# Tails of three weight matrices and of their gradients handled in pairs of slices, in an attention and gated-unit backward kernel

## The chip, the cores and the metric

The kernel runs on one core of one Trainium2 chip. A core has a matrix engine (PE, whose weight loads the profile calls PEld), a vector engine (DVE), a scalar engine (ACT), GpSimd (POOL), and SyncE (SP), which here only issues transfers. 16 DMA engines move data between the chip's memory (HBM) and the core's on-chip buffers. A tile in SBUF has 128 partitions; matrix products land in PSUM and have to be copied out of it by ACT or DVE. The metric is the time in device microseconds of one execution; the median of three runs is compared.

## The reference

One decode step (one token, two sequences) of an attention block and a bilinear gated unit that run side by side on the same normalised input, and the gradients of all of it. `D` is 576, there are 32 query heads and 16 key/value heads of 128, 4096 cached positions, and 4608 hidden columns in the gated unit.

```python
def _A_ref(x, k_cache, v_cache, wq, wo):
    q = (x @ wq).reshape(B, Sq, Hq, Dh).transpose(0, 2, 1, 3)
    k = jnp.repeat(k_cache, rep, axis=1)
    v = jnp.repeat(v_cache, rep, axis=1)
    scores = jnp.einsum("bhqd,bhkd->bhqk", q, k) * (Dh ** -0.5)
    p = _softmax(scores, axis=-1)
    o = jnp.einsum("bhqk,bhkd->bhqd", p, v)
    return o.transpose(0, 2, 1, 3).reshape(B, Sq, Hq * Dh) @ wo
def _B_ref(x, w_gate, w_up, w_down):
    g = jnp.einsum("bsd,df->bsf", x, w_gate)
    u = jnp.einsum("bsd,df->bsf", x, w_up)
    return jnp.einsum("bsf,fd->bsd", g * u, w_down)
...
xn = _layernorm(A_x)
out = A_x + _A_ref(xn, A_k_cache, A_v_cache, A_wq, A_wo) + _B_ref(xn, B_w_gate, B_w_up, B_w_down)
```

The kernel returns `out` and the gradients, for a given `grad_out`, of `x`, both caches, `wq`, `wo`, `w_gate`, `w_up` and `w_down`. The caches and their gradients are by far the largest: 33.6 MB each, in bf16. In all 92.5 MB are read and as much is written.

## The kernel before

**Attention.** The 16 key/value heads are taken in 8 groups of two heads; a group with its two sequences makes two steps, 16 in all. A step loads two K tiles and two V tiles of 1 MB (`load_kv`, L997), transposes them in 32x32 blocks on DVE into tiles called X (`turn`, L421), takes scores and the softmax (`softmax`, `dscore`), contracts with the untransposed tiles (`contract`), and makes the gradients of K and V as outer products, which are cast out of PSUM into 1 MB tiles and stored (`head_outer`; the casts are `cp`, L425 on ACT and L427 on DVE; the store is `put`, L652, issued by SP). K and V tiles, X tiles and store tiles all come out of one ring of 16 tiles, `big`, with a cap for each use: 8 for K and V, 13 for X, 5 for stores.

**Weights of a group.** `load_w` loads four heads' columns of `wq` (512 columns) and rows of `wo` into tiles `ww`. `wq` has 576 rows, that is four blocks of 128 and a tail of 64. The blocks are one transfer of 512 KB (L1015). The tail's 64 rows by 512 columns are split into two halves of 256 columns, one on partitions 0 to 63 and one on 64 to 127 of the same `ww` tile (L1011, 64 KB; for group 0 on SP's queue, else on POOL's). `group_front` multiplies them with the normalised input, `xs`. `xs` holds the input's tail twice, with zeros in the other half (blocks 4 and 5), so that a tile with something else on its other half can be multiplied with it. `group_back`, after both steps of the group, makes the gradients of `wo` (`rows_outer`) and of `wq` (`cols_outer` for the 512 rows, `tail_outer` for the 64 of the tail) and transposes `wq` (L955, one instruction over 2304 columns taken as 1152 32-bit ones) to find what flows back to the input (`dxn`, L630 and L635; added into `accx`, L964).

**Gated unit.** `mlp` runs over nine slices of 512 columns, 0 to 8. A slice's `gu` tile holds four blocks of gate, four of up, and one block in which partitions 0 to 63 hold gate's tail and 64 to 127 up's (L1033, two transfers of 64 KB, besides two of 512 KB at L1030; all on POOL's queue). There is one `gu` buffer; it is released (L824) when the slice's columns have been transposed for the flow back to the input, the tail among them into `Xt`. `w_down` goes to a `ww` tile on SP's queue (L1037).

**Gradients of the tails.** `tail_outer` has one or two right-hand sides. For gate and up it puts gate on partitions 0 to 63 and up on 64 to 127 of a `tl` tile (two buffers) and stores each with 64 KB (L652); for `wq` only partitions 0 to 63 are used:

```python
def ev(e, o):
    cp(e, st[0:64 * nw, 256 * A:256 * A + 256].rearrange("p (a f) -> p a f", a=2), o[0:64 * nw, :, 0:P])
return mms, (0.053, 0.104), 256, ev
```

Each tail is evicted in two pieces of 256 columns.

**Order.** Nothing is scheduled at run time. While the program is built, `Order` runs every part of the work as a stream that asks for engine time, buffers and transfers, with a modelled duration for each; among streams that could start on an engine within `SLACK` of the first, the one with the lowest priority number goes first. That fixes the order of instructions on each engine, and of the transfers on SP's and POOL's queues. The priority of a stream is `STEP * s + PR[name]`, with additions for the first two steps (`HEAD`) and the last two (`TAIL`); `DMA` models a transfer's time, `CAP` the shares of the ring, `MLP0` and `MLPD` when the slices' weights are loaded, counted in K and V loads, `BIAS` the choice between ACT and DVE for a cast. An instruction that comes up before its data are there waits, and so does all behind it on its engine or queue.

**Start and end.** `front` loads `x` and `grad_out` (2.2 KB each, ACT's queue) into `xy`, a tile of its own that is kept to the end; there `rows_add` and `rows_put` add them to the results of `final_out` and `final_dx` and store these through it (L1327 to L1329).

## Time and profile before

| | before |
|---|---|
| median of 3 runs | 482.37 us (481.89 to 482.74) |
| span of the profiled execution | 482.5 us |
| PE, PEld busy | 377.9 us (78%), 212.1 us (44%) |
| DVE busy | 349.8 us (73%), 658 instructions |
| ACT busy | 345.6 us (72%), 529 instructions |
| POOL busy | 248.5 us (51%), 356 instructions |
| moved by DMA | 185.93 MB in 33,444 packets, 385 GB/s over the span |
| PE clock granted, mean | 0.654 |

The profiled execution is a run of its own; its span differs from the median by 0.1 us, so what is read from it can be set against the runs directly. The page cuts the span into 40 slices of 12 us. The DMA engines' busy tenths in them show at a glance where transfers run (9 is 90% or more), and the line under it how much they moved:

```profile
DMA  8998999999999989999999999999999999999894
GB/s 298 385 404 326 415 392 422 386 384 397 422 412 378 370 332 328 394 417 402 416 403 409 367 401 420 398 412 422 407 396 421 421 413 394 401 399 376 300 410 164
```

A transfer is cut into packets that its 16 engines work through; the packet records give start, length and size of each. The page lists what the queues' transfers were; the median from issue to landing is the last number:

```profile
out_dram<-big SPq DMA_DIRECT2D x64, 1024.0 KB, 12.1
out_dram<-big POOLq DMA_DIRECT2D x26, 512.0 KB, 11.1
out_dram<-tl POOLq DMA_DIRECT2D x26, 64.0 KB, 8.4
gu<-in_B_w_gate_dram POOLq DMA_DIRECT2D x9, 64.0 KB, 11.7
ww<-in_A_wq_dram POOLq DMA_DIRECT2D x7, 64.0 KB, 9.4
```

### The profile page before, as it was taken

The page shows a single profiled execution, that of the slowest core. Times are in us where ns is not written, and L with a number is a line of the kernel's source. Part 1 is how long each engine was busy: PE and PEld are TensorE (multiplying, and loading weights), DVE is VectorE, ACT ScalarE, POOL GpSimd, SP SyncE. Part 2 cuts the span into 40 slices and gives each one's busy share as a digit, 9 for nine tenths or more (in the row PEclk, how much of TensorE's full clock was granted, in tenths as well). Part 3 has the DMA queues.
Part 4 walks back from the last instruction along what each step waited for, and adds up shares of the span by engine and source line. Part 5 has one row for each costly group of instructions (what it writes and reads, how often), then busy time and mean ns, then how long its engine had stood idle before and what let it go on. Part 6 is the DMA issues. An engine that isn't in the chain of part 4 may idle for free. (4 is left out here: it accounts for less than half of the span.)

```text
span 482.5 us, 14582 instructions
## 1 busy us (share of the span) xinstructions
PE 377.9 (78%) x6122; PEld 212.1 (44%) x6122; DVE 349.8 (73%) x658; ACT 345.6 (72%) x529; POOL 248.5 (51%) x356
## 2 busy tenths in 40 slices
PE   0577978668962899879989898787896887598996
PEld 0444545433631544535553554444452544334544
DVE  6678857866766868677577888687676788298872
ACT  6059976578871688976658974789786982498992
POOL 6176803874057663551557624865715863265601
PEclk9999585675855656655555755767575765568575
DMA  8998999999999989999999999999999999999894
GB/s 298 385 404 326 415 392 422 386 384 397 422 412 378 370 332 328 394 417 402 416 403 409 367 401 420 398 412 422 407 396 421 421 413 394 401 399 376 300 410 164
DMA packets 33444, 185.93 MB, mean 385 GB/s; under 512 B 5034, under 2 KB 5170, under 8 KB 16994
## 3 DMA queue, kind: packets, MB, share of 16 engines
q1 hardware_dynamic: 18714, 131.22, 67.8%
q0 software_dynamic: 14656, 53.77, 29.5%
q8 instruction: 48, 0.79, 0.6%
q14 instruction: 18, 0.15, 0.1%
q10 hardware_dynamic: 8, 0.00, 0.0%
HBM read 92.48 MB, written 92.48 MB: 383 GB/s over the span
## 5 line engine op out<-in xcount | busy, mean ns | idle before, releaser
L425 ACT CAST big<-ps_o 128x1024 bf16<-128x1024 f32 (+1 forms) x324 | 288.4, 962 | 47.1 <-PE ps_o L1129 33.8
L421 DVE STREAM_TRANSPOSE big<-big 128x1024 f32<-128x1024 f32 x128 | 152.8, 1219 | 15.8 <-DMA out_dram<-big 11.7
L1095 POOL TENSOR_TENSOR BD<-vr,mask 128x2048 bf16<-128x2048 bf16 x32 | 115.3, 3602 | 33.6 <-ACT vr L425 16.6
L1107 PE MATMUL ps_m<-big,W 128*32 128x128 bf16 x2048 | 59.6, 283 | 10.2 <-POOL W L1072 6.1
L427 DVE CAST big<-ps_o 128x1024 bf16<-128x1024 f32 (+1 forms) x52 | 59.5, 1145 | 9.7 <-PE ps_o L1129 3.6
L1129 PE MATMUL ps_o<-BD,pp 32*128 32x512 bf16 x256 | 54.3, 533 | 14.9 <-ACT big L425 6.6
L1107 PEld LDWEIGHTS <-W 128*32 128x32 bf16 x2048 | 47.2, 125 | 28.4 <-issue 19.5
L1129 PE MATMUL ps_o<-BD,dd 32*128 32x512 bf16 x256 | 51.8, 544 | 6.1 <-ACT big L425 5.1
L652 POOL DMA_DIRECT2D out_dram<-big x43 | 33.4, 777 | 39.1 <-ACT big L425 25.3
L1072 POOL COPY W<-rep 32x16 bf16<-32x16 bf16 x128 | 24.5, 192 | 56.1 <-DVE rep L873 51.2
L421 DVE STREAM_TRANSPOSE big<-ww 128x1152 f32<-128x1152 f32 x25 | 34.0, 1358 | 6.2 <-DMA out_dram<-big 5.9
L1284 PE MATMUL ps_m<-big,pp 128*32 128x512 bf16 x256 | 32.2, 607 | 2.2 <-DVE accx L834 1.3
L623 POOL COPY wt<-wm 64x128 bf16<-64x128 bf16 (+1 forms) x34 | 8.9, 261 | 44.6 <-DVE wm L617 43.6
L1129 PEld LDWEIGHTS <-pp 32*128 32x128 bf16 x256 | 12.3, 99 | 39.0 <-issue 34.2
L1284 PE MATMUL ps_m<-big,dd 128*32 128x512 bf16 x256 | 27.1, 512 | 0.8 <-DVE accx L834 0.3
L421 DVE STREAM_TRANSPOSE big<-gu 128x1024 f32<-128x1024 f32 x18 | 21.8, 1224 | 1.6 <-PE ps_m L1107 0.8
L1129 PEld LDWEIGHTS <-dd 32*128 32x128 bf16 x256 | 10.7, 99 | 27.7 <-issue 22.7
L652 POOL DMA_DIRECT2D out_dram<-tl x26 | 14.4, 557 | 15.4 <-ACT tl L425 5.7
L1294 ACT ACTIVATE osb<-ps_m 128x512 bf16<-128x512 f32 x15 | 9.2, 611 | 16.5 <-PE ps_m L1284 16.5
L630 PE MATMUL ps_m<-big,wm 128*32 128x128 bf16 x416 | 14.2, 299 | 5.5 <-DVE big L421 4.4
L672 PEld LDWEIGHTS <-xnr 32*128 32x128 bf16 x416 | 14.4, 111 | 8.0 <-issue 6.4
L672 PE MATMUL ps_o<-hb,xnr 32*128 32x128 bf16 x288 | 15.2, 251 | 2.7 <-ACT big L425 1.4
(210 smaller groups left out, 561.7 us busy)
## 6 DMA issues: line engine op xcount, KB each, us to landing
out_dram<-big SPq DMA_DIRECT2D x64, 1024.0 KB, 12.1
big<-in_A_k_cache_dram SPq DMA_DIRECT2D x28, 1024.0 KB, 13.5
big<-in_A_v_cache_dram SPq DMA_DIRECT2D x28, 1024.0 KB, 18.0
out_dram<-big POOLq DMA_DIRECT2D x26, 512.0 KB, 11.1
out_dram<-big POOLq DMA_DIRECT2D x17, 576.0 KB, 9.4
ww<-in_B_w_down_dram SPq DMA_DIRECT2D x9, 576.0 KB, 15.7
ww<-in_A_wo_dram POOLq DMA_DIRECT2D x8, 576.0 KB, 15.1
gu<-in_B_w_gate_dram POOLq DMA_DIRECT2D x9, 512.0 KB, 12.1
```

The source lines that it names most:

```text
L421: nc.vector.transpose(out, in_)
L425: nc.scalar.copy(out, in_)
L427: nc.vector.tensor_copy(out=out, in_=in_)
L630: nc.tensor.matmul(dp[32 * q:32 * q + 32, 0:P], lhsT=view(Wm[:], 0, P, 8 * pos(q, s), [[1, 32]]), rhs=view(X, 0, P, xoff(q, s), [[xstep, 4 ...
L652: (nc.gpsimd if engine == "POOL" else nc.sync).dma_start(dst, src)
L672: nc.tensor.matmul(o[:, aa, dc * P:(dc + 1) * P], lhsT=xnr[32 * a:32 * a + 32, dc * P:(dc + 1) * P], rhs=rhs(a), start=True, stop=True)
L1072: nc.gpsimd.tensor_copy(view(W_t[t][w][:], 32 * a, 32, 6 + 8 * a, [[G * WW, 4], [WW, G], [1, 2]]), view(rep_t[grp[g]["qs"]][:], 32 * a, 32 ...
L1095: nc.gpsimd.tensor_tensor(BD_t[i][:], view(vr_t[v][:], 0, P, 0, [[0, 16], [1, Dh]]), view(mask16[:], 0, P, 0, [[1, 16], [0, Dh]]), ALU.mult)
L1107: nc.tensor.matmul(sc[32 * cq:32 * cq + 32, :], lhsT=view(W[:], 0, P, (be * G + l) * WW + 6 - 4 * c2 - 2 * l, [[1, 32]]), rhs=view(X[:], 0 ...
L1129: nc.tensor.matmul(o[:, k, :], lhsT=pr2[32 * c4:32 * c4 + 32, :], rhs=BD[32 * c4:32 * c4 + 32, 8 * l + 4 * h2:8 * l + 4 * h2 + 4, :], star ...
L1284: nc.tensor.matmul(ct[32 * j:32 * j + 32, :], lhsT=view(rT, 0, P, 4 * c + 2 * l, [[1, 32]]), rhs=kv_t[kvS[s][t][l]][:, Dh * c:Dh * (c + 4) ...
L1294: nc.scalar.activation(ob, cs, AF.Copy, scale=SCALE)
```

## The change

The tails of `wq`, `w_gate` and `w_up`, and those of their gradients, are no longer handled per slice (or group) but per pair of slices: the even one's 64 rows lie on partitions 0 to 63 and the odd one's on 64 to 127, each with all its 512 columns, in tiles of their own (`gtl` and `wqt` for weights, `tg` and `tq` for gradients). A pair's tails are loaded with the even slice and stored with the odd one, 128 KB a transfer; the ninth slice of the gated unit has no partner and keeps 64 KB. For two right-hand sides `tail_outer` now evicts 64 partitions by 512 columns, not 128 by 256. The transposes of the tails become two instructions each. `Store(9, None, 0)` is a counter that never runs out, since the store is now spawned by `tail_outer` itself. `xy` goes: `x` and `grad_out` are first loaded into a tile of the shared ring, which is released once they have been used, and again near the end (`final_load`), after the last K or V load has been issued, into an X tile. `gs`, `hT` and `gT` have one buffer instead of two. All parameters of the order are others.

```diff
@@ -286,27 +286,26 @@
 def DMA(engine, cost, nbytes, row=8192):
-    packet = 0.0375 * row + 9.0
-    return ("dma", engine, cost, 0.08 + nbytes / 16e3 * packet / row, packet)
+    packet = 0.0364 * row + 8.0
+    return ("dma", engine, cost, 0.02 + nbytes / 16e3 * packet / row, packet)
-CAP = {"kv": 8, "X": 13, "st": 5}
-MLP0, MLPD = 0, 7.51
+CAP = {"kv": 8, "X": 15, "st": 5}
+MLP0, MLPD = 0.53, 7.43
-WQ0, WO0 = 0, 1
+WQ0, WO0 = 0, -2
-BIAS = 0.52
-SLACK = {"PE": 0.07, "ACT": 0.09, "DVE": 0.43, "POOL": 8.93, "SP": 17.19}
+BIAS = 0.572
+SLACK = {"PE": 0.07, "ACT": 0.11, "DVE": 0.33, "POOL": 6.62, "SP": 18.36}
...
@@ -374,16 +373,19 @@
-    gu_t = tiles("gu", NGU, [P, 9 * FS])
+    gu_t = tiles("gu", NGU, [P, 8 * FS])
+    gtl_t = tiles("gtl", 1, [P, 2, FS])
+    wqt_t = tiles("wqt", 2, [P, FS])
     ww_t = tiles("ww", NWW, [P, WB])
-    tl_t = tiles("tl", 2, [P, FS])
+    tg_t = tiles("tg", 1, [P, 2, FS])
+    tq_t = tiles("tq", 1, [P, 1, FS])
-    gs_t = [const.tile([P, 2, P], FP32, name=f"gs{i}") for i in range(2)]
-    hT_t = [const.tile([P, FC, 32], BF16, name=f"hT{i}") for i in range(2)]
-    gT_t = [const.tile([P, 8, 32], BF16, name=f"gT{i}") for i in range(2)]
+    gs = const.tile([P, 2, P], FP32, name="gs")
+    hT = const.tile([P, FC, 32], BF16, name="hT")
+    gT = const.tile([P, 8, 32], BF16, name="gT")
...
@@ -523,10 +525,8 @@
-    xy = const.tile([2, 2 * D], BF16, name="xy")
-
     def front():
-        xb, yb = xy[:, 0:D], xy[:, D:2 * D]
+        xb, yb = st_t[2][0:2, D:2 * D], st_t[2][0:2, 2 * D:3 * D]
...
-        for j in range(1, 4):
+        for j in (1, 3):
             yield REL("st", j)
...
+        yield REL("st", 2)
...
@@ -706,36 +707,49 @@
-    def tail_outer(rhss, dsts, p, events=()):
-        i = yield ACQ("tl")
-        st = tl_t[i]
-        nw = len(rhss)
-        parts = [(d, st[64 * w:64 * w + 64, 0:FS], 64 * FS * 2) for w, d in enumerate(dsts)]
-        store = Store(2, put("POOL", parts, "tl", i, events, 4096), p)
+    def tail_outer(rhss, hh, pair, tag, tl, out, n0, last, p, done):
+        if pair.get(tag) is None:
+            pair[tag] = yield ACQ(tag)
+        i = pair[tag]
+        st, nw = tl[i], len(rhss)
+        if hh:
+            pair[tag] = None
 
         def mk(A):
             def mms(o):
                 for w, rhs in enumerate(rhss):
                     for aa in range(2):
-                        a = 2 * A + aa
-                        nc.tensor.matmul(o[64 * w:64 * w + 64, aa, 0:P], lhsT=xnr[32 * a:32 * a + 32, 512:576],
-                                         rhs=rhs(a), start=True, stop=True)
+                        nc.tensor.matmul(o[64 * hh:64 * hh + 64, aa, P * w:P * (w + 1)],
+                                         lhsT=xnr[32 * (2 * A + aa):32 * (2 * A + aa) + 32, 512:576],
+                                         rhs=rhs(2 * A + aa), start=True, stop=True)
 
             def ev(e, o):
-                cp(e, st[0:64 * nw, 256 * A:256 * A + 256].rearrange("p (a f) -> p a f", a=2), o[0:64 * nw, :, 0:P])
-            return mms, (0.053, 0.104), 256, ev
+                cp(e, view(st[:], 64 * hh, 64, 2 * P * A, [[P, 2], [FS, nw], [1, P]]),
+                   view(o[:], 64 * hh, 64, 0, [[512, 2], [P, nw], [1, P]]))
+            return mms, (0.053 * nw, 0.104), 2 * P * nw, ev
+        if hh:
+            parts = [(d[512:576, n0 - FS:n0 + FS].rearrange("p (h n) -> h p n", h=2), st[:, w, :], P * FS * 2)
+                     for w, d in enumerate(out)]
+        else:
+            parts = [(d[512:576, n0:n0 + FS], st[0:64, w, :], 64 * FS * 2) for w, d in enumerate(out)]
+        ends = [Event(), Event()]
+
+        def one(A):
+            yield from unit(*mk(A), Store(9, None, 0))
+            yield SET(ends[A])
         for A in range(2):
-            yield SPAWN(unit(*mk(A), store), p)
-
-    def mlp(i, Lgu, Ld, gs_slot, wd_slot):
-        gu, wd = gu_t[gs_slot], ww_t[wd_slot]
+            yield SPAWN(one(A), p)
+        yield WAIT(*ends)
+        yield SET(done)
+        if hh or last:
+            yield SPAWN(put("POOL", parts, tag, i, (), 4096)(), p + PR["store"])
+
+    def mlp(i, Lgu, Ld, gs_slot, tl_slot, wd_slot):
+        gu, gtl, wd, hh = gu_t[gs_slot], gtl_t[tl_slot], ww_t[wd_slot], i % 2
         hs = yield ACQ("hb")
-        hb, gs, hT, gT = hb_t[hs], gs_t[hs], hT_t[hs], gT_t[hs]
+        hb = hb_t[hs]
...
@@ -743,10 +757,10 @@
-                k = 4 * w + dc if dc < 4 else 8
+                src = gu[:, FS * (4 * w + dc):FS * (4 * w + dc + 1)] if dc < 4 else gtl[:, w, :]
                 for a in range(4):
-                    nc.tensor.matmul(ug[32 * a:32 * a + 32, 1 - w, :], lhsT=xs[:, dc if dc < 4 else 4 + w, :],
-                                     rhs=gu[:, FS * k + P * a:FS * k + P * (a + 1)], start=(dc == 0), stop=(dc == 4))
+                    nc.tensor.matmul(ug[32 * a:32 * a + 32, 1 - w, :], lhsT=xs[:, dc if dc < 4 else 4 + hh, :],
+                                     rhs=src[:, P * a:P * (a + 1)], start=(dc == 0), stop=(dc == 4))
...
-        yield SPAWN(tail_outer([lambda a, w=w: hb[32 * a:32 * a + 32, 1 + w, :] for w in range(2)],
-                               [out[512:576, f0:f0 + FS] for out in (out_6, out_7)], po, (E[3],)), po)
+        yield SPAWN(tail_outer([lambda a, w=w: hb[32 * a:32 * a + 32, 1 + w, :] for w in range(2)], i % 2, pairs_,
+                               "tg", tg_t, (out_6, out_7), f0, i == NFS - 1, po, E[3]), po)
...
@@ -819,9 +833,12 @@
-        yield DVE(0.4)
-        t32(pairs(Xt[:]), pairs(gu[:, 4096:4608]))
+        for w in range(2):
+            yield DVE(0.37)
+            t32(pairs(Xt[64 * w:64 * w + 64, :]), pairs(gtl[64 * hh:64 * hh + 64, w, :]))
         yield REL("gu", gs_slot)
+        if hh or i == NFS - 1:
+            yield REL("gtl", tl_slot)
...
@@ -846,14 +863,14 @@
-                c0 = dc * FS + h * P if dc < 4 else 4 * FS + (h % 2) * P
-                nc.tensor.matmul(qp[:, h, :], lhsT=wq[:, c0:c0 + P], rhs=xs[:, dc if dc < 4 else 4 + h // 2, 0:2],
+                w = wq[:, dc * FS + h * P:dc * FS + (h + 1) * P] if dc < 4 else wqt[:, h * P:(h + 1) * P]
+                nc.tensor.matmul(qp[:, h, :], lhsT=w, rhs=xs[:, dc if dc < 4 else 4 + g % 2, 0:2],
                                  start=(dc == 0), stop=(dc == 4))
...
@@ -924,7 +941,8 @@
-        yield SPAWN(tail_outer([lambda a: R[32 * a:32 * a + 32, 1, :]], [out_4[512:576, n0:n0 + FS]], po, (E[2],)), po)
+        yield SPAWN(tail_outer([lambda a: R[32 * a:32 * a + 32, 1, :]], g % 2, pairs_, "tq", tq_t, (out_4,), n0, False,
+                               po, E[2]), po)
...
@@ -951,9 +969,15 @@
-        yield DVE(1.37)
-        t32(pairs(X[:, 0:WB]), pairs(wq[:]))
+        yield DVE(1.25)
+        t32(pairs(X[:, 0:4 * FS]), pairs(wq[:, 0:4 * FS]))
         yield REL("ww", st["wq"])
+        hh = 64 * (g % 2)
+        for k in range(2):
+            yield DVE(0.24)
+            t32(pairs(X[64 * k:64 * k + 64, 4 * FS:4 * FS + 256]), pairs(wqt[hh:hh + 64, 256 * k:256 * k + 256]))
+        if hh:
+            yield REL("wqt", st["wqt"])
...
@@ -1007,10 +1033,13 @@
-                yield DMA("POOL" if i else "SP", 0.6, 128 * 256 * 2, 4096 if i else 512)
-                (nc.gpsimd if i else nc.sync).dma_start(ww_t[w][:, 4 * FS:WB],
-                                                        A_wq[512:576, n0:n0 + FS].rearrange("p (h n) -> h p n", h=2))
-                yield ("lset", st["Lq"])
+                if i % 2 == 0:
+                    st["wqt"] = grp[i + 1]["wqt"] = r = yield ACQ("wqt")
+                    yield DMA("POOL" if i else "SP", 0.78 if i else 0.36, 128 * FS * 2, 4096 if i else 1024)
+                    (nc.gpsimd if i else nc.sync).dma_start(
+                        wqt_t[r][:], A_wq[512:576, n0:n0 + 2 * FS].rearrange("p (h n) -> h p n", h=2))
+                    yield ("lset", st["Lq"])
+                    yield ("lset", grp[i + 1]["Lq"])
...
@@ -1024,20 +1053,27 @@
+            if i % 2 == 0:
+                tails["gtl"] = yield ACQ("gtl")
+            gtl = gtl_t[tails["gtl"]]
...
-                yield DMA("POOL", 0.6, 64 * FS * 2, 4096)
-                nc.gpsimd.dma_start(gu[64 * w:64 * w + 64, 8 * FS:9 * FS], Wsrc[512:576, f0:f0 + FS])
+                if i == NFS - 1:
+                    yield DMA("POOL", 0.6, 64 * FS * 2, 4096)
+                    nc.gpsimd.dma_start(gtl[0:64, w, :], Wsrc[512:576, f0:f0 + FS])
+                elif i % 2 == 0:
+                    yield DMA("POOL", 0.78, 128 * FS * 2, 4096)
+                    nc.gpsimd.dma_start(gtl[:, w, :], Wsrc[512:576, f0:f0 + 2 * FS].rearrange("p (h n) -> h p n", h=2))
             yield ("lset", Lgu)
...
-            yield SPAWN(mlp(i, Lgu, Ld, g, d), pr("mlp", (MLP0 + i * MLPD) / 4))
+            yield SPAWN(mlp(i, Lgu, Ld, g, tails["gtl"], d), pr("mlp", (MLP0 + i * MLPD) / 4))
...
+    Exy, xys = Event(), []
+
+    def final_load():
+        yield WAIT(issued[4 * NS - 1])
+        i = yield ACQ("X")
+        xys.append(X_t[i])
+        for n, src in enumerate((A_x, grad_out)):
+            yield DMA("SP", 0.36, 2304, 1152)
+            nc.sync.dma_start(X_t[i][0:2, D * n:D * (n + 1)], src.rearrange("b s d -> (b s) d"))
+        yield ("lset", Exy)
-        yield WAIT(Eprep, *acc_E)
+        yield WAIT(Eprep, Exy, *acc_E)
...
+    od.spawn(final_load(), PR["fin"])
```

Line numbers in the text are those of the kernel before.

## The prediction

> **What bounds the kernel now.** I read the page's queue shares first, then stages of the span, then waits.
>
> ```profile
> q1 hardware_dynamic: 18714, 131.22, 67.8%
> q0 software_dynamic: 14656, 53.77, 29.5%
> q8 instruction: 48, 0.79, 0.6%
> q14 instruction: 18, 0.15, 0.1%
> ```
>
> Columns: packets, MB, share of the 16 DMA engines' span. q1 carries what SP issues, q0 what POOL issues. Together 98.0% of 482.5 us, that is 472.9 us of packet time: the transfers fill the span, while PE, DVE and ACT are busy for 78, 73 and 72%. So the time changes only with packet time or with stretches in which the DMA engines have nothing to do. The stages (busy of PE, PEld, DVE, ACT, POOL, then granted clock, DMA share, GB/s) show where those are:
>
> ```profile
> 0.00:6.00 6.00, 0.00 (x0) 0.00 (x0) 4.86 (x32) 3.80 (x7) 5.38 (x14) 1.00 0.69 215
> 36.00:44.00 8.00, 5.81 (x117) 3.23 (x116) 7.21 (x14) 8.00 (x13) 6.08 (x5) 1.00 0.83 278
> 162.00:180.00 18.00, 16.80 (x264) 9.93 (x264) 13.05 (x26) 11.78 (x22) 10.50 (x9) 0.50 0.89 335
> 440.00:458.00 18.00, 16.12 (x254) 9.38 (x258) 16.59 (x29) 16.42 (x24) 10.94 (x9) 0.65 0.80 310
> 458.00:472.00 14.00, 13.08 (x191) 6.40 (x180) 9.55 (x18) 12.05 (x16) 0.68 (x3) 0.74 1.00 409
> 472.00:482.50 10.50, 6.39 (x69) 4.04 (x68) 2.67 (x12) 3.53 (x6) 2.11 (x3) 0.50 0.36 127
> ```
>
> Length times (1 - DMA share): 1.9, 1.4, 2.0, 3.6, 0 and 6.7 us, in all 15.6 us without transfers. (Elsewhere the share comes to 1.01 or 1.02, since packets of the two queues overlap a little; hence 15.6 rather than 482.5 - 472.9 = 9.6.) The first is the start, the last the closing chain. The three in between, 7.0 us, are what another order can win; the reader should see that ACT and DVE are full in two of them and PE in the third (16.80 of 18 us, at a clock of 0.50).
>
> **1. Packet time.** Tails move in 52 transfers of 64 KB: 26 stores (L652 from tl), 18 loads of gate and up (L1033), 8 of wq (L1011, the first by SP, all others by POOL). The packet records of the trace, taken along each queue in order of issue, give 0.18 us of 16-engine time for a store from tl, 0.20 and 0.18 for the gate and up tails, 0.22 for a wq tail; a 512 KB transfer takes 1.37 to 1.44, an eighth of which is 0.175. The tails take 9.9 us in all; at the wide rate 52 x 0.175 = 9.1. The gain lies between 0 (packets stay at 4 KB) and 0.8; I take 0.4, the middle, as the new shape is in no row. After the change there are 27 such POOL issues (3 + 10 loads, 10 + 4 stores) against 51 before, besides the one by SP. Each POOL issue adds 16 packets of 4 B at 9.4 ns, so 24 x 16 x 9.4 ns / 16 = 0.23 us less. Before each POOL wq tail there are also 112 packets of 32 B at 14.8 ns (0.10 us; 7 times, 0.73 us). If these belong to rows of 512 B, all 0.73 goes; if to the two-half source (h, p, n), which gate and up loads and the pair stores now have too (23 transfers), they become 2.4 us, 1.7 more. I take 0, as L1011 has both traits and cannot tell them apart. Sum -0.6, bounds -1.8 and +1.5.
>
> **2. Fewer POOL issues ahead of the weight loads.**
>
> ```profile
> L652 POOL DMA_DIRECT2D out_dram<-tl x26 | 14.4, 557 | 15.4 <-ACT tl L425 5.7
> L1011 POOL DMA_DIRECT2D ww<-in_A_wq_dram x7: 847/871/887, 36.1 to 375.7; - x7
> ```
>
> The page's groups (busy us, mean ns) and the listing of the tail load's line (least/median/most ns). With 18 gate and up issues of 550 ns this is 14.4 + 9.9 + 6.1 = 30.4 us of POOL; the new 27, 128 partitions at 0.78 like the wide stores, 0.87 for wq and 0.55 for the four half tails of the last slice, come to 8 x 0.78 x 2 + 4 x 0.78 + 4 x 0.55 + 3 x 0.87 = 20.4. POOL is 51% busy, so the 10 us count only where a load waits behind them. That is so at groups 1 and 3: POOL issues the wq tail at 36.1 and 159.1 us, the wide wq load 0.87 later, and q0's first data packet starts at 40.6 and 163.6 after the small ones, inside the stages with shares 0.83 and 0.89. Odd groups load no tail any more. I take 0.87 for the earlier issue at one of the two places, as SP's stores in the same stages wait for ACT anyway (SP waited 14.4 us for one cast before 36.1): -0.9; bounds 0 and -1.7.
>
> **3. The order.** All priorities, slacks and the DMA model that places issues are new, and the copies in X may hold 15 of the 16 shared tiles, not 13. Of the 7.0 us, 0.9 is spent in step 2; of the other 6.1 I take a quarter, -1.5. Bounds: -6.1, and +4.6, which is one more gap like that of 440 to 458 and half one of 162 to 180. The quarter is a choice: 3.6 of the 6.1 lie in the closing stage, where evictions (PSUM casts L425, L427) keep ACT and DVE at 16.4 and 16.6 of 18 us and no order makes them shorter.
>
> **4. Vector work added.** By the groups with shapes kept apart:
>
> ```profile
> L425 ACT CAST tl<-ps_o 128x256 bf16<-128x256 f32 x13 | 4.9, 414 | 1.0 <-PE ps_o L721 0.9
> L425 ACT CAST osb<-ps_m 128x512 bf16<-128x512 f32 x15 | 9.0, 601 | 8.3 <-PE ps_m L1284 6.9 <-ACT big L425 1.3
> L421 DVE STREAM_TRANSPOSE Xt<-gu 128x256 f32<-128x256 f32 x9 | 3.7, 407 | 0.0
> L421 DVE STREAM_TRANSPOSE dof<-ps_m 128x128 f32<-128x128 f32 x8 | 2.4, 298 | 0.6 <-PE ps_m L945 0.6
> L421 DVE STREAM_TRANSPOSE big<-ww 128x1152 f32<-128x1152 f32 x25 | 34.0, 1358 | 6.2 <-DMA out_dram<-big 5.9 <-DMA ww<-in_B_w_down_dram 0.2
> L421 DVE STREAM_TRANSPOSE big<-big 128x1024 f32<-128x1024 f32 x128 | 152.8, 1219 | 15.8 <-DMA out_dram<-big 11.7 <-DMA big<-in_A_k_cache_dram 2.8 <-PE ps_m L1107 1.1
> ```
>
> A gate/up tail is now evicted as 64 partitions by 512 columns, not 128 by 256: 18 x (601 - 414) = 3.4 us. Its transpose is done twice: 9 x 407 = 3.7. wq is transposed as 1024 and twice 128 columns: 8 x (1219 + 2 x 298 - 1358) = 3.7. In all 10.8 us on two engines that together idle for 269 of 965; the cover is the transfers, so outside the end I cost it at nothing. Uncovered, it would be half of it, 5.4. At the end one piece is on the chain: the last wq transpose at 469.6 us releases L635, L964 (473.3) and the chain of waits that closes the span. That is +0.45; bounds 0 (another order) and +1.2 (with the last slice's two casts and transpose, 2 x 0.19 + 0.41, in the same stage and not hidden).
>
> **5. Costed at nothing.** One buffer instead of two for gs, hT and gT: there is one gu buffer, so the next slice's products (L748) already wait until its transposes have released gu (L824), after all three have been read; without that the wait would be the whole slice's. One tg and one tq: pairs are two slices or groups apart (some 100 us) and a tail store lands 8.4 us after its issue. x and grad_out again: two loads of 2.2 KB queued on SP behind loads of K and V; what stands behind them on SP is stores, and their wait is for an X tile, of which there are 16 with the last V load issued at 422. If that wait fell among stores, the longest such wait that SP's queue shows for a tile is 18.4 us, which would be rival B. Tile 2 of the shared ring is freed some us later at the start, while the cap of 8 on K and V holds loads back anyway. SP's first wq tail moves 128 KB rather than 64: counted in 1.
>
> **Sum.** 482.5 - 0.6 - 0.9 - 1.5 + 0.45 = 479.95. The profiled execution is 0.1 above the median of the runs, 482.37, so I predict 479.8.
>
> **Rivals.** *B, slower: stores pile up behind the last load.* In the trace the last V load lands at 440.9 us; after it SP issues 7 more stores of 1 MB and POOL 5 wide ones. A 1 MB store needs four casts of 1024 columns, 1.03 us on ACT or 1.22 on DVE; on both together 4 / (1/1.03 + 1/1.22) = 2.2 us. In this stage no other cover is left: DMA share 0.80 and then 0.36. An order that loads sooner, with more tiles for copies, leaves more stores behind the last load, at 2.2 us each. The point is the second one: with order gain nought, 482.4 - 1.5 + 0.45 + 2 x 2.2 = 485.8; with one, 483.6. For it speaks that SP already waits for casts longer than for anything:
>
> ```profile
> SPq L652 <- ACT big L425: 154.3, 43, 14.7
> SPq L652 <- DVE big L427: 96.4, 17, 16.8
> SPq L997 <- DMA out_dram<-big: 31.8, 10, 18.4
> ```
>
> (total us, times, longest). Against it: POOL and SP are freed a little, and the old order leaves 3.6 us there to win. *C, no change.* Packets of 8 KB take 309 ns in the median but 325 in the mean: 16,384 x 16 ns / 16 = 16 us are lost to stretching, and what steps 1 to 3 free may only be stretched again: 482.4 + 0.45 less at most 0.9, that is 482. *D, more than forecast: half-partition transfers slow the whole machine.* 44 of the 52 tails touch only 64 partitions. If these ran at half rate, each would take 0.35 us instead of 0.175, and wide ones would save 44 x 0.175 = 7.7: 479.95 + 0.4 - 7.7 = 472.7, with what is left unpaired (4 of them) 473.4. Against it stand 0.18 to 0.20 us per tail. [...]
>
> **Chances.** Forecast 0.53, its own range 476 to 481.3. B 0.31, spread from 483.4 to 490. C 0.12. D 0.04. About 0.2%, or 1 us, is what a measurement can tell from no change here; so faster 0.57, same 0.12, slower 0.31. With every low end of the steps the sum is 482.4 - 1.8 - 1.7 - 6.1 = 472.8; with every high end 482.4 + 1.5 + 4.6 + 1.2 = 489.7. They hardly fall together: 474.5 to 487 leaves out half of D, the best of the forecast and about a quarter of B, some 0.16.
>
> **What would show it.** Step 1: 51 POOL tail issues become 27, the total packet time falls by 0.5 us or so, and the 32-byte packets (under 512 B, now 5034) show which trait makes them. Step 2: no dip of the DMA share where groups 1 and 3 load wq. Step 3: idle transfers in the middle under 5 us. Step 4: DVE and ACT together up by some 11 us, POOL down by 10. B: more than 7 SP stores after the last V load, and a share under 0.80 in the 40 us behind it. What makes the prediction wrong is above all step 3, which no row of the old trace can price: a new long gap anywhere in the middle outweighs everything else.

## The result, and the profile after

| | before | after |
|---|---|---|
| median of 4 runs each, same chip | 482.13 us (481.45 to 482.74) | 516.72 us (513.31 to 518.11) |
| ratio, 95% interval | | 1.0705 (1.0667 to 1.0743) |
| span of the profiled execution | 482.5 us | 511.4 us (its whole time 513.31) |

The kernel became 7% slower; 479.8 was forecast, and the range ended at 487. The profiled execution of after is the fastest of its four. A span is also 1.8 to 2.0 us shorter than the whole time of its execution, so the 482.5 of before belongs to an execution of some 484.4 us (an estimate from the other runs), not to one at the median. For both reasons the traces differ by 28.9 us where the medians differ by 34.6. Runs more than 1.5% above the fastest of their kernel (499.91 and 493.57 us below) count as slow, and the ratios leave them out, while medians and ranges have all runs.

The page of after: engines, the 40 slices of DMA, the queues.

```profile
span 511.4 us, 14579 instructions
PE 375.0 (73%) x6122; PEld 212.2 (41%) x6122; DVE 358.6 (70%) x677; ACT 350.5 (69%) x535; POOL 239.4 (47%) x332
...
DMA  8995999995999999999999999999979969999796
GB/s 295 364 371 192 340 411 423 322 380 185 338 342 381 409 419 399 352 365 386 421 346 395 421 413 398 402 379 405 423 296 418 415 232 373 397 424 418 273 405 219
DMA packets 37421, 186.00 MB, mean 364 GB/s; under 512 B 9022, under 2 KB 9162, under 8 KB 20970
...
q1 hardware_dynamic: 18722, 131.29, 65.1%
q0 software_dynamic: 18624, 53.76, 29.0%
```

Two things differ. The slices have holes (192, 185, 232 GB/s) where before had none but at its two ends, and q0 has 3968 packets more for the same bytes. The stages (busy of PE, PEld, DVE, ACT, POOL; granted clock, DMA share, GB/s) show the holes:

```profile
38.00:46.00 8.00, 7.53 (x123) 3.71 (x119) 7.17 (x10) 6.45 (x9) 5.25 (x5) 1.00 0.32 127
...
116.00:126.00 10.00, 9.20 (x183) 5.95 (x179) 9.07 (x16) 5.40 (x8) 3.60 (x1) 0.61 0.37 129
372.00:380.00 8.00, 7.42 (x121) 3.56 (x119) 6.48 (x11) 7.70 (x12) 6.64 (x6) 0.50 0.69 250
410.00:417.00 7.00, 3.95 (x70) 2.20 (x70) 2.53 (x5) 4.32 (x5) 3.41 (x7) 0.50 0.33 108
470.00:511.40 41.40, 32.16 (x490) 17.19 (x486) 27.28 (x55) 29.86 (x44) 10.39 (x13) 0.71 0.81 308
```

The first four lose 5.4, 6.3, 2.5 and 4.7 us (length times 1 - share). The closing 41.4 us lose 7.9; the closing 42.5 of before lost 3.6 + 6.7 = 10.3, so the loss is not at the end. The first hole, in slices of 0.2 us:

```profile
DMA  7955322322312102101003100100000000009399
GB/s 333 497 228 246 164 123 123 164 123 123 164 82 123 82 41 123 82 41 82 41 41 123 82 41 41 82 41 0 0 0 0 0 0 0 0 0 492 164 655 328
```

This is no pause but a staircase. 41 GB/s is one packet of 8 KB in 0.2 us: first half of the 16 engines work, then five, three, two, one, then none. All but one of the packets here are SP's (q1). The last of them before the hole belong to the two K loads issued at 24.9 and 27.2 us. These land at 41.6 and 44.1, when the last engine has finished, though the first ones were done before 39. Nothing new is queued behind them, since the work had stopped before: the up tail of the first slice, issued by POOL at 5.9 us, landed only 32.0 us later, and PE waited for it until 37.9, ACT and DVE behind PE. The four casts for the next store begin at 40.7, and SP issues it at 44.5. From 22 to 37 us POOL's queue had 1.8 packets of 4 KB under way in the mean.

The packet records put a number on that, when one counts how many packets are under way at each moment (16 at most, since packets of the two queues overlap a little in the records: 472.9 us of packet time in before, 465.7 so counted):

| us of the span | before | after | after, cut transfers in two (first experiment) |
|---|---|---|---|
| all 16 engines' work, as if spread evenly | 465.7 | 477.0 | 462.6 |
| idle: no engine works | 5.0 | 11.8 | 8.2 |
| idle: 1 to 8 of 16 work (share that idles) | 7.9 | 17.0 | 11.3 |
| idle: 9 to 15 work | 3.9 | 5.7 | 3.5 |

Of 28.9 us more span 17.7 are idle engines (34.5 against 16.8). The rest, 11.3, is the engines' work: 2.8 are the tiny packets explained below (3.5 against 0.7), and most of what is left is packets of the same size that took longer, those of 8 KB 331.0 ns in the mean against 325.2.

Which transfers do this? The list of issues of after (size; median us from issue to landing) and two waits at the new tiles (total us, times, longest), with the first of them in before as the last line:

```profile
out_dram<-tg POOLq DMA_DIRECT2D x8, 128.0 KB, 11.9
gtl<-in_B_w_gate_dram POOLq DMA_DIRECT2D x4, 128.0 KB, 20.4
gtl<-in_B_w_up_dram POOLq DMA_DIRECT2D x4, 128.0 KB, 25.6
out_dram<-tq POOLq DMA_DIRECT2D x4, 128.0 KB, 11.7
```

```profile
ACT gs L765 <- PE ps_m L762: 27.3, 3, 14.5
...
PE ps_m L762 <- DMA gtl<-in_B_w_up_dram: 8.1, 3, 4.5
...
ACT gs L751 <- PE ps_m L748: 5.5, 6, 1.9
```

The gate and up tails, the last loads of a slice, land 20 and 26 us after issue, the 512 KB load issued just ahead of the gate tail after 15.1. The slice's first product (L762) waits for them, and ACT behind it. One such landing is the longest piece of the chain that ended last (start us, us):

```profile
201.73 25.43 DMA gtl<-in_B_w_up_dram
```

The new transfers have one trait in common: their DRAM side is `rearrange("p (h n) -> h p n", h=2)`, two halves of 64 rows each. I call them cut transfers: 12 loads and 12 stores. 23 of them are POOL's, and 23 times 224 packets of 16 bytes is 5152; before had 7 with 112 of 32 bytes, 784. I call these packets fillers, as the data of a cut transfer are all in its 32 packets of 4 KB. That accounts for the growth in packets under 512 B: 5034, and 4368 more fillers, less 24 x 16 = 384 for the POOL issues saved, is 9018; the page has 9022.

### The profile page after: what moved, and what is told of

It reads as the page before. It is cut to its first block, busy times and chain, and to the rows that moved or that the text cites. A ratio compares the mean times of both kernels' runs of the same rounds, so it can differ in the third digit from the quotient of the medians.

```text
span 511.4 us, 14579 instructions
## 1 busy us (share of the span) xinstructions
PE 375.0 (73%) x6122; PEld 212.2 (41%) x6122; DVE 358.6 (70%) x677; ACT 350.5 (69%) x535; POOL 239.4 (47%) x332
## 4 chain that ended last, share of the span: by engine, by line
DMA 30%; PE 18%; ACT 10%; DVE 8%; issue 5%; POOL 3%; ACTq 0%; POOLq 0%; DVEq 0%
DMA out_dram<-big 22%; ACT big L427 8%; DMA gtl<-in_B_w_up_dram 5%; PE ps_m L1143 4%; PE ps_o L1165 4%; DVE big L423 4%; DMA ww<-in_A_wq_dram 3%; DVE big L429 2%; PE ps_m L1320 2%; PE ps_m L906 1%; PE ps_m L780 1%; POOL out_dram L653 1%; POOL W L1108 1%; ACT tg L427 1%; PE ps_m L631 1%
## 5 line engine op out<-in xcount | busy, mean ns | idle before, releaser
L423 DVE STREAM_TRANSPOSE big<-big 128x1024 f32<-128x1024 f32 x128 | 154.5, 1225 | 25.5 <-DMA out_dram<-big 13.2
L429 DVE CAST big<-ps_o 128x1024 bf16<-128x1024 f32 (+1 forms) x51 | 60.1, 1181 | 15.1 <-PE ps_o L1165 9.9
L1143 PE MATMUL ps_m<-big,W 128*32 128x128 bf16 x2048 | 61.5, 288 | 4.9 <-DVE oT L1340 2.5
L1165 PE MATMUL ps_o<-BD,pp 32*128 32x512 bf16 x256 | 51.5, 540 | 16.2 <-ACT big L427 13.6
L1165 PE MATMUL ps_o<-BD,dd 32*128 32x512 bf16 x256 | 47.6, 508 | 12.7 <-ACT big L427 9.2
L423 DVE STREAM_TRANSPOSE big<-ww 128x1152 f32<-128x1152 f32 (+1 forms) x25 | 33.0, 1320 | 11.9 <-DMA out_dram<-big 8.5
L1320 PE MATMUL ps_m<-big,pp 128*32 128x512 bf16 x256 | 30.9, 573 | 1.0 <-DMA big<-in_A_v_cache_dram 0.5
L765 ACT COPY gs<-ps_m 128x256 f32<-128x256 f32 x9 | 3.5, 390 | 27.4 <-PE ps_m L762 27.3
L762 PEld LDWEIGHTS <-xs 128*32 128x32 bf16 x360 | 8.9, 131 | 30.6 <-issue 24.5
L906 PE MATMUL ps_m<-big,Wdy 128*128 128x128 bf16 x144 | 15.0, 285 | 8.1 <-DVE big L423 6.8
L767 DVE TENSOR_TENSOR hb<-gs,ps_m 128x128 bf16<-128x128 f32 x9 | 2.5, 277 | 25.9 <-ACT gs L765 25.9
## 6 DMA issues: line engine op xcount, KB each, us to landing
out_dram<-big SPq DMA_DIRECT2D x64, 1024.0 KB, 10.8
gu<-in_B_w_gate_dram POOLq DMA_DIRECT2D x9, 512.0 KB, 15.1
```

What stands on the lines that cost most here:

```text
L423: nc.vector.transpose(out, in_)
L429: nc.vector.tensor_copy(out=out, in_=in_)
L906: nc.tensor.matmul(dp, lhsT=Wdy[:, e, 2 * k:2 * k + P], rhs=view(X[:], 0, P, 64 * k + e, [[D, GH], [2, 32]]), start=(k == 0 and e == 0), s ...
L1143: nc.tensor.matmul(sc[32 * cq:32 * cq + 32, :], lhsT=view(W[:], 0, P, (be * G + l) * WW + 6 - 4 * c2 - 2 * l, [[1, 32]]), rhs=view(X[:], 0 ...
L1165: nc.tensor.matmul(o[:, k, :], lhsT=pr2[32 * c4:32 * c4 + 32, :], rhs=BD[32 * c4:32 * c4 + 32, 8 * l + 4 * h2:8 * l + 4 * h2 + 4, :], star ...
L1320: nc.tensor.matmul(ct[32 * j:32 * j + 32, :], lhsT=view(rT, 0, P, 4 * c + 2 * l, [[1, 32]]), rhs=kv_t[kvS[s][t][l]][:, Dh * c:Dh * (c + 4) ...
```

## The experiments

The theory (T1): a cut transfer is worked by two of the 16 engines alone, and the other 14 get 16 filler packets each (14 x 16 = 224). Each of the two gets 64 KB at once, falls behind, and whatever is queued behind it lands only when the slowest engine has worked it off. The main rival (T2) is step 3 of the prediction: the new order is at fault. Others: the vector work added (T3), the single buffers, the 15 tiles.

**The cut transfers alone.** After's order and everything else stay; each cut transfer is issued as two of 64 KB.

```diff
-                    (nc.gpsimd if i else nc.sync).dma_start(
-                        wqt_t[r][:], A_wq[512:576, n0:n0 + 2 * FS].rearrange("p (h n) -> h p n", h=2))
+                    for h in range(2):
+                        (nc.gpsimd if i else nc.sync).dma_start(
+                            wqt_t[r][64 * h:64 * h + 64, :], A_wq[512:576, n0 + FS * h:n0 + FS * (h + 1)])
```

and likewise for the gate and up loads and for the stores from tg and tq.

> The changed kernel; each of its 24 tail transfers over both halves (4 of wq, 8 of gate and up, 12 stores) is issued as two transfers of 64 KB, one for each half; order and vector work stay. Theory T1 (a transfer cut into two halves is worked off by 2 of the 16 engines, which then lag, and what follows waits for them): no packets of 16 B, no stretch in which only 2 to 5 engines work, time 476 to 486 us. Rival T2 (the new order and the 15 tiles for copies leave the gaps): gaps at 38 to 46, 116 to 126 and 410 to 417 us stay, time 508 to 520. Rival T3 (the added vector work): 508 to 520, with gaps elsewhere.

Measured 487.79 us (484.92 to 490.8), 1.0097 of before (1.0064 to 1.013): 28.9 of 34.6 us are gone, though 487.8 is above the 476 to 486 that T1 forecast. The page, the landing of the gate and up tails, and the same stages as above:

```profile
DMA packets 32667, 185.92 MB, mean 383 GB/s; under 512 B 4268, under 2 KB 4408, under 8 KB 16216
...
q1 hardware_dynamic: 18752, 131.29, 67.0%
q0 software_dynamic: 13840, 53.68, 28.9%
...
gtl<-in_B_w_gate_dram POOLq DMA_DIRECT2D x9, 64.0 KB, 15.4
gtl<-in_B_w_up_dram POOLq DMA_DIRECT2D x9, 64.0 KB, 18.1
```

```profile
38.00:46.00 8.00, 6.66 (x109) 3.98 (x105) 6.38 (x14) 5.68 (x9) 2.50 (x4) 0.50 0.80 326
...
116.00:126.00 10.00, 8.02 (x142) 4.14 (x136) 7.62 (x14) 8.96 (x13) 5.89 (x11) 0.50 0.93 354
372.00:380.00 8.00, 5.98 (x71) 3.38 (x65) 7.39 (x11) 5.27 (x11) 6.89 (x10) 0.71 1.02 422
410.00:417.00 7.00, 6.50 (x124) 3.68 (x121) 4.37 (x11) 6.18 (x13) 1.98 (x4) 0.83 1.03 416
440.00:458.00 18.00, 13.89 (x258) 7.95 (x253) 13.81 (x27) 13.94 (x22) 8.07 (x9) 0.68 0.60 231
```

The filler packets are gone, and the shares go from 0.32, 0.37, 0.69, 0.33 to 0.80, 0.93, 1.02, 1.03. The tails land after 15 and 18 us instead of 20 and 26. What is left over before is one new dip, at 440 to 458 (0.60; before 0.80). By the table above the two traces, 25.9 us apart, differ by 11.5 us of idle engines (34.5 against 23.0) and by 14.4 of the engines' work; the fillers are 3.5 of that, and packets of 8 KB took 324.2 ns in the mean instead of 331.0. Why packets take longer in after no run shows, and it is not peculiar to cut transfers: in the kernel with BIAS 0.52 below, which has none, they took 329.8.

**Loads only, stores only.** The same edit for the 12 loads, and for the 12 stores.

> The changed kernel; only the 12 tail loads over both halves are issued as two. T1: the loads' lag reaches work that waits for weights and for the K and V tiles behind them, and the first gap (38 to 46 us, 5.7 us without transfers) goes; 484 to 502 us, the gain near the loads' share of the 24 (half of 34 us), rather more. T2 and T3: 508 to 520.

> The changed kernel; only the 12 pair stores are issued as two. T1: 492 to 508 us, and with the run in which only the loads are apart the two gains add up to about the gain of both. T2 and T3: 508 to 520.

Measured 499.06 (492.24 to 499.91), 1.0279 (1.0194 to 1.0364), and 503.87 (501.88 to 508.46), 1.0412 (1.0361 to 1.0462). Loads are worth 516.72 - 499.06 = 17.7, stores 12.9; together 30.6, against 28.9 for both at once. The four runs with the loads in two spread over 7.7 us, so this agrees with a cost that is a sum over the transfers, but only to within some us.

**The old order under the new transfers, and with pairs apart.** First, all order parameters of before in after; then the first experiment's edit added to that.

```diff
-CAP = {"kv": 8, "X": 15, "st": 5}
+CAP = {"kv": 8, "X": 13, "st": 5}
...
-BIAS = 0.572
+BIAS = 0.52
...
```

> The changed kernel with all parameters of the order before (priorities, slacks, caps, transfer model); the pair transfers stay over both halves. T1: it stays slow, 500 to 525 us. T2: 480 to 487. T3: 500 to 525 too, so that this run tells T2 apart from the others, not T1 from T3.

> The changed kernel with all parameters of the order before and with the pair transfers issued as two halves. The run with halves apart and the new order took 487.8 us; what is left of it over 482.5 is either the order's or that of the pairs themselves (two more transposes, wider casts, single buffers). If the order's: 480 to 484 here. If the pairs': 486 to 491.

Measured 517.98 (515.16 to 521.65), 1.0722 (1.0653 to 1.079), and 489.41 (487.02 to 490.87), 1.0125 (1.0087 to 1.0162). The old order does not help, and in it the cut transfers cost 517.98 - 489.41 = 28.6, the 28.9 of the new order again. By what was expected above, 489.4 also puts the rest over before on the pairs rather than on the new order. The page of the first of the two has the holes in other slices (235, 141):

```profile
GB/s 299 367 363 235 255 414 411 307 405 371 374 403 392 378 402 405 383 274 385 418 416 409 419 407 346 402 407 399 417 410 418 141 269 359 421 417 418 244 304 199
```

T2 falls as the cause of the 34.6 us.

**One transfer by itself.** A kernel that leaves out the computation: four cut loads of a wq tail, one after the other, each awaited before the next; then four pairs of 64 KB; the same for stores; then loads with a 1 MB K load on SP.

```diff
+    def cut(h):
+        nc.gpsimd.dma_start(small[:], A_wq[512:576, 1024 * h:1024 * h + 1024].rearrange("p (h n) -> h p n", h=2))
+    def apart(h):
+        for k in range(2):
+            nc.gpsimd.dma_start(small[64 * k:64 * k + 64, :], A_wq[512:576, 1024 * h + FS * k:1024 * h + FS * (k + 1)])
```

> Leaves out the whole computation; only transfers, one after the other on an idle core, each step waited for: 4 loads of 128 KB over both halves in one transfer, 4 as two of 64 KB; 4 stores of either kind; then 4 times a load of either kind on POOL's queue followed by a 1 MB load of K on SP's. T1 (2 of 16 engines): the single load keeps at most 2 engines busy for 16 packets of some 160 ns each, about 2.6 us of packets against 0.4 us for the pair, with 224 packets of 16 B for each; and the 1 MB load behind it lands about 2 us later than behind the pair. If the cut itself cost nothing, both kinds would take 0.4 us of packets and the 1 MB loads land alike.

The stretches in which packets ran, for one cut load, one pair of loads, one cut store, one pair of stores (us; busy of DVE and POOL; clock, DMA share, GB/s), and the issues:

```profile
10.90:13.50 2.60, 0.00 (x0) 0.00 (x0) 1.00 0.17 50
29.70:31.10 1.40, 0.00 (x0) 0.00 (x0) 1.00 0.31 94
46.80:50.40 3.60, 0.00 (x0) 0.00 (x0) 1.00 0.13 36
68.20:69.20 1.00, 0.00 (x0) 0.00 (x0) 1.00 0.59 131
```

```profile
small<-in_A_wq_dram POOLq DMA_DIRECT2D x3, 128.0 KB, 4.7
small<-in_A_wq_dram POOLq DMA_DIRECT2D x8, 64.0 KB, 2.5
out_dram<-small POOLq DMA_DIRECT2D x4, 128.0 KB, 5.8
out_dram<-small POOLq DMA_DIRECT2D x8, 64.0 KB, 2.0
```

This is the theory in one line. A cut load takes 2.6 us at a share of 0.17, which is 2.7 of 16 engines, and a cut store has 0.13, or 2.1 engines. In the kernel before a packet of 8 KB takes 309 ns in the median, 26.5 GB/s for an engine, so 50 GB/s is 1.9 engines. Of the packets of 4 KB, 2.0 are under way at once in the mean of a cut load. One cut load alone lands 4.7 us after its issue, each transfer of a pair 2.5 after its own; for stores it is 5.8 and 2.0. The part with a K load tells nothing, as the K load was under way before POOL's transfer began; it landed 5.1 us after issue either way.

**A load queued behind.** Transfers alone again, the 1 MB K load on POOL's own queue right behind one tail, then behind two.

```diff
+    for f, n in ((cut, 1), (apart, 1), (cut, 2), (apart, 2)):
+        for r in range(3):
+            for h in range(n):
+                f(h)
+            nc.gpsimd.dma_start(wide[:], kview[0, r])
+            step()
```

> Leaves out the whole computation; only loads on POOL's queue, each step waited for: three times one tail load of 128 KB over both halves in one transfer with a 1 MB load of K right behind it on the same queue; three times the same with the tail as two transfers of 64 KB; then both with two tails ahead; then twice eight tail loads alone, of either kind. T1: two engines reach the 1 MB load some 2.3 us after the others (16 packets of 160 ns, less the 2 that each engine has anyway), so that it lands about 2 us later behind one such tail than behind the pair, and no more than that behind two, if the second goes to other engines. Eight at once take 3 to 5 us if each goes to two other engines, some 21 if all go to the same two; eight pairs 3 us.

The issues behind one cut tail, then behind one pair:

```profile
wide<-in_A_k_cache_dram POOLq DMA_DIRECT2D x3, 1024.0 KB, 7.7
small<-in_B_w_up_dram POOLq DMA_DIRECT2D x3, 128.0 KB, 6.3
```

```profile
wide<-in_A_k_cache_dram POOLq DMA_DIRECT2D x3, 1024.0 KB, 5.2
small<-in_B_w_up_dram POOLq DMA_DIRECT2D x6, 64.0 KB, 2.2
```

Counted from its own issue, the 1 MB behind a cut tail lands 2.5 us later than behind a pair, though the tail is an eighth of its size. Behind two it is 7.9 against 5.4, again 2.5 and not 5.0. So two in a row seem to go to different engines, though which ones the records do not say. The time of eight in a row decides nothing: 16 cut ones took 22.7 us, between the 42 (16 x 2.6) that one pair of engines for all would take and the 10 or so expected of a spread, as POOL takes some 0.8 us to issue one (843 ns in the median for the gate tails of after) and the second eight wait for the tiles of the first. But their packet records do: 6.9 packets of 4 KB are under way at once in the mean, up to 11, where a single cut load has 2.0, up to 3. They were spread over more than one pair of engines.

**The old kernel's own cut transfers.** Before's eight wq tails have the two-half source too, at 64 KB. Here each is two transfers of 256 columns.

```diff
-                (nc.gpsimd if i else nc.sync).dma_start(ww_t[w][:, 4 * FS:WB],
-                                                        A_wq[512:576, n0:n0 + FS].rearrange("p (h n) -> h p n", h=2))
+                for h in range(2):
+                    (nc.gpsimd if i else nc.sync).dma_start(ww_t[w][64 * h:64 * h + 64, 4 * FS:WB],
+                                                            A_wq[512:576, n0 + 256 * h:n0 + 256 * (h + 1)])
```

> The kernel before, in which the wq tail of each of the 8 groups, already a transfer over two halves, is issued as two. T1: the kernel before pays for the same thing in its own 8 transfers, half as large each: the dips at 39 to 42 and 162 to 166 us go, 477 to 481.5 us; no packets of 32 B. Rival (what the kernel before loses there is its order's): 481.5 to 484.

Measured 483.72 (481.29 to 485.65), 1.0019 (0.9996 to 1.0041): the gain that T1 expected did not come. The stages of the prediction in this kernel:

```profile
36.00:44.00 8.00, 7.93 (x122) 4.76 (x122) 7.47 (x14) 7.62 (x11) 5.90 (x5) 1.00 0.98 315
162.00:180.00 18.00, 16.02 (x265) 10.10 (x264) 13.32 (x27) 12.00 (x22) 11.04 (x10) 0.59 0.91 336
440.00:458.00 18.00, 16.30 (x251) 8.86 (x248) 16.35 (x29) 16.43 (x23) 9.73 (x10) 0.69 0.66 250
```

The dip at 36 goes (0.83 to 0.98, 1.2 us), that at 162 hardly moves, and the time comes back at 440 to 458 (0.80 to 0.66, 2.5 us). What eight cut transfers of half the size cost here is thus not visible in the time; these stages are from one trace each.

**The rest of 5.3 us: vector work, buffers, order.** The first experiment still stands 5.3 us above before. Before was given, one at a time, the vector work of after (tail transposes in two halves, tail evictions per 64 partitions); the single buffers; all order parameters of after; and these with the wq tails in two.

```diff
-        t32(pairs(Xt[:]), pairs(gu[:, 4096:4608]))
+        for w in range(2):
+            t32(pairs(Xt[64 * w:64 * w + 64, :]), pairs(gu[64 * w:64 * w + 64, 4096:4608]))
```

```diff
-    gs_t = [const.tile([P, 2, P], FP32, name=f"gs{i}") for i in range(2)]
+    gs_t = [const.tile([P, 2, P], FP32, name="gs")] * 2
```

> The kernel before in its own order, with more vector work in place: the gate and up tails' transposes in two halves, the wq transposes as 1024 and twice 128 columns, and each eviction of a gate/up tail as two of 64 partitions by 256 columns (about 0.37 us more for each of 18, twice what the change adds). About 14 us more of DVE and ACT time, no other transfer. If the vector work makes the 5 us that the changed kernel with halves apart is still slower (T3, reduced to that rest): 486 to 490. If it is hidden behind the transfers as the prediction had it: 482 to 484.

> The kernel before in its own order, with one buffer instead of two for gs, hT and gT, as in the change. Costed at nothing in the prediction, since the single gu buffer already keeps the slices apart: 482 to 484. If a slice did wait for the one before: 485 or more.

> The kernel before with all parameters of the new order (priorities, slacks, caps with 15 tiles for copies, transfer model), its transfers and vector work unchanged. With the three other corners (old order and old tails 482.3, old order and pairs apart 489.4, new order and pairs apart 487.8) it tells the order's share from the pairs'. If the pairs themselves cost the rest and the order next to nothing: 481 to 485. If an order only suits the tails it was made for: 486 to 491, as in the opposite corner.

> The kernel before with all parameters of the new order, and its 8 wq tail transfers issued as two halves. With the old order the halves made no difference (482.3 and 483.7 us); with the new order and the wq tails over both halves it took 506.0. If these 8 transfers are what the new order cannot bear (T1): 484 to 492. If the new order is simply unfit for tails in slices, whatever the transfers: 500 to 508.

| before with | median us (lowest to highest) | ratio (95%) |
|---|---|---|
| the vector work | 485.52 (482.82 to 488.48) | 1.0034 (1.0 to 1.0068) |
| single buffers | 482.17 (478.96 to 485.21) | 0.998 (0.9945 to 1.0015) |
| the new order | 506.04 (503.08 to 508.41) | 1.0459 (1.0408 to 1.051) |
| the new order, wq tails in two | 503.37 (501.96 to 503.66) | 1.0428 (1.0396 to 1.0461) |

The vector work, 16.6 us more of DVE and ACT time here where after has 13.7, costs 0 to 3.3 us, in between the two ranges that were expected; the buffers cost nothing. The new order in the old kernel costs 22 us, more than either alternative allowed for. The wq tails over two halves are not the reason: issuing them in two brings 2.7, and the intervals of the two ratios overlap. So an order can cost tens of microseconds in a kernel that it was not made for, but it need not: the old order under the pairs, with the cut transfers in two, costs 1.6 (489.4 against 487.8). Which of its parameters matter was asked with four single edits: BIAS (before, 0.572), X (before, 15), and in the first experiment's kernel BIAS 0.52 and X 13.

```diff
-BIAS = 0.52
+BIAS = 0.572
```

> The kernel before with one parameter of its order nudged: the bias between ACT and DVE for a cast, 0.572 instead of 0.52, the value of the new order. If an order's accident weighs several us: 485 to 500. If only a wholly different order does: 481 to 484.

> The kernel before with up to 15 of the 16 shared tiles for copies instead of 13. Prediction's rival B let more copies starve loads and stores: 485 to 490 then. If the cap binds seldom: 481 to 485.

> The changed kernel with halves apart, the bias 0.52 instead of 0.572. If the rest of 5.3 us is the accident of the fit, another order moves it either way by as much: 482 to 498. If it belongs to the pairs: 486.5 to 489.

> The changed kernel with halves apart, 13 tiles for copies instead of 15. If the 15 tiles make the rest: 482 to 484.5. If the fit of the order does: anything from 484 to 498, and above 487.8 rather than below.

| | median us (lowest to highest) | ratio to before (95%) |
|---|---|---|
| before, BIAS 0.572 | 493.68 (492.62 to 498.95) | 1.0256 (1.0187 to 1.0324) |
| before, X 15 | 483.01 (481.56 to 486.94) | 1.0024 (0.9995 to 1.0053) |
| cut transfers in two, BIAS 0.52 | 496.52 (493.45 to 500.85) | 1.0271 (1.0209 to 1.0334) |
| cut transfers in two, X 13 | 487.86 (484.04 to 493.57) | 1.0097 (1.0066 to 1.0129) |

The number of tiles is worth nothing that these runs can tell. BIAS costs each kernel about 9 to 11 us when it takes the other's value (493.7 - 482.5; 496.5 - 487.8). A nudge of one parameter of the order can thus be worth some 10 us. That weakens what the run in the old order said for the pairs, and a rest of 5.3 us, less the vector work's 0 to 3.3, can't be split further by such runs. It stays open how much of it belongs to pairs of slices as such. No version tried was faster than before by more than the noise.

## Why the prediction was wrong

**The step that failed** is step 1, and in it the price of a transfer over two halves: taken as 0, with 1.7 us as the worst case, it was 28.9. The reasoning there was that a transfer costs its packets' time divided by 16 engines; the fillers of the two-half source were seen (112 packets of 32 B on L1011), named as a possible trait of all 23 POOL transfers, and priced at 2.4 us in all, 1.7 more than before, at most: "I take 0". The fillers did come with the two halves and not with rows of 512 B, and were 3.5 us of 16-engine time, as there are 224 to a transfer. But they are the mark of the trouble and not the trouble. Fourteen groups of 16 fillers would fit fourteen engines that get none of the data, with 64 KB for each of the other two; the records name no engine, but one cut transfer alone has a share of 0.13 to 0.17, that is 2.1 to 2.7 engines. The price is landing time: 2.5 us late for what is queued behind one (the kernel of transfers), 28.9 and 28.6 us for 24 of them in two orders, or 1.2 us apiece, against 0.35 us of 16-engine time for 128 KB. How the 28.9 comes about is shown only in part: of the 25.9 us between the two traces, 11.5 are engines that idle and 3.5 fillers, while longer packets, most of the rest, are unexplained. A sign was in view, as 112 fillers are 14 x 8, but step 1 did not ask over how many engines a transfer is spread. That question would have been the rival that the prediction lacked. Why a transfer of two halves keeps only some two engines at work, and how another number of halves would fare, no run shows.

**Packet time** was to fall by 0.6. It rose from 472.9 to 484.8 us (94.8% of 511.4). The stretching of packets that rival C counted on (those of 8 KB from 325.2 to 331.0 ns in the mean) is part of it, but with the sign against the change. With the cut transfers in two, which but for wq are the 64 KB transfers of before, the engines' work is 462.6 against 465.7, on one trace each; the old fillers of 0.7 are part of that. What a wide tail would save without the cut was not tried.

**Step 2** had POOL right (248.5 to 239.4, 9.1 less; 10 forecast) and the dip at 36 us wrong. It blamed the issue time ahead of the wide load. Before with its wq tails in two issues one more transfer there and has no dip, so the cut tail ahead of the load is the likely cause at 36 us. At 162 us, with the same kind of tail, the share went only from 0.89 to 0.91, and the cause of that dip stays open. In after the place is the worst hole, at a share of 0.32.

**Step 3** put -1.5 on the order, with bounds of -6.1 and +4.6. A single parameter, BIAS, moves either kernel by about 10 us, so the bounds were too narrow, but the order is not what made after slow: the old one gives 518.0.

**Step 4** forecast 10.8 us more on DVE and ACT: 358.6 + 350.5 less 349.8 + 345.6 is 13.7. The evictions are 17 on ACT at 577 ns (601 taken), the wq transposes 1227 + 2 x 296 as taken, and the gate/up halves 430 where 407 was taken:

```profile
L423 DVE STREAM_TRANSPOSE Xt<-gtl 64x256 f32<-64x256 f32 x18 | 7.7, 430 | 0.3
```

That transfers hide it, as costed, holds to within 0 to 3.3 us. **Step 5**, the single buffers and the shared tiles, holds as far as it was tried, in the kernel before: 482.17, and 483.01 with X 15.

**The rivals.** B: 6 SP stores of 1 MB are issued after the last V load has landed (474.9 us), against 7, and the closing 41.4 us have a share of 0.81; stores do not pile up. C expected no change and fell. D fell too: the first experiment brings 64-partition transfers back, and the engines' work falls from 477.0 to 462.6. No run shows the half rate that D's 7.7 us are worked out from; the 64-partition tails of before took 0.18 to 0.20 us of 16-engine time each, not 0.35.

## What to carry to other kernels

Before merging two transfers into one, measure the merged one alone: a cut load here, of two halves of 64 rows, had 2.0 packets under way at once in the mean and landed 4.7 us after its issue, and two issues of half the size, 2.5 us each, were better than one. Layouts other than two halves were not tried. Price a transfer by its landing and by what is queued behind it (1 MB landed 2.5 us later), not by its packets over 16 (0.35 us here); an unexplained run of tiny filler packets in the record, here 224 of 16 bytes to a transfer, is the sign. A fixed order can be worth tens of microseconds to the kernel that it was made for, so judge a change of structure in both orders, as here, where the cut transfers cost 28.9 and 28.6.

## What the runs showed that I had not expected

Two cut tails in a row delay the load behind them by 2.5 us, no more than one does. In the kernel with the cut transfers in two, a lag remains that no cut transfer explains: the last V load, which POOL issues at 421.2 us, lands at 446.9, after 25.7 us; that of before, issued at 422.0, at 440.9, after 18.8. A transfer has 16 completions in the trace. For POOL's transfers issued from 409 to 429 us, the last one comes 7.4 to 9.9 us behind the one before it, against 2.4 to 4.7 in before. If each of the 16 completions stands for one engine, which the trace does not say, one engine trails all others on that queue. The dip at 440 to 458 (shares 0.60 and 0.80) comes with it. What delays the last completion was not found.
